# Nine rooms for the raw weight pieces of a gated linear attention and SwiGLU kernel, four of them fetched at once

## The chip, the cores and the metric

The kernel runs on one core of a Trainium2 chip. A time is the device time of one execution in microseconds (us); several executions of the same kernel are run and the median is told. Beside them stands one execution that was profiled: it has a time of its own, and a span, from the first to the last instruction, that is a little shorter. Everything read from a profile belongs to that one execution.

## The reference, cut to what matters

```python
# q, k, v, a_re, a_im: (4, 8, 768, 48) f32; weights arrive as float64
mag = sqrt(a_re**2 + a_im**2); scale = min(mag, 0.999) / (mag + 1e-6)
a = (a_re + 1j * a_im) * scale
for t in range(768):                       # per batch and head
    S = a[t][:, None] * S + outer(k[t], v[t])
    y[t] = q[t] @ real(S)
x = y as (3072, 384)                       # tokens x (heads * 48)
xn = x / sqrt(mean(x*x) + 1e-6) * rms_g
out = (silu(xn @ w_gate) * (xn @ w_val)) @ w_out   # 384 -> 1536 -> 384
```

## The kernel before

The 3072 tokens are 24 chunks of 128. The recurrence is computed by chunk: the running products of the gates are turned into a magnitude (products, square roots) and a phase (arctan, running sum, sine and cosine), keys and queries are scaled and rotated by them ("rot0" to "rot3": four multiplications), and then each chunk is a small attention: scores (`s_ps`, L1064), transposed keys (`kt_ps`, L1085), the carried state (`state_ps`, L1107) and outputs (`y_ps`, L1136). The output is normalised (`ss_ps` twice, a root on GpSimd, called POOL, at L1171) and written as `xT`.

Gates are computed for *units*: units 0 and 1 are one chunk each, every later unit is two chunks. After its four rotations a unit's rows are moved from one layout in SBUF to another by DMAs (L876, `kr` and `qr`; the four moves are `moved0` to `moved3`), and its first scores wait for all four. Units 0 and 1 issue their `qr` moves on the POOL queue, all else goes on SP's queue.

The feed-forward works on *groups* of two chunks. A gate tile ("tile" in the text: `gv_ps`, L1212) is six matmuls with a gate weight and six by a value weight as the profile counts them; ACT applies silu to the one half (L1216) and VectorE, called DVE, multiplies (`hT<-gv_ps`, L610). There are twelve tiles in a group, 144 in all, and three PSUM buffers for them. Groups 0 and 1 are projected by `wo` directly (L1239), later ones with seven products instead of eight (L1290), whose weight sums `combine` computes.

The weights arrive in 64-bit form and are narrowed in the kernel. They come in 18 *pieces* of 768 KB: pieces 0 to 11 are, in turn, gate and value weights of six column blocks (two tiles need the two pieces of a block), pieces 12 to 17 are `wo`. `fetch` (L944) issues a DMA for each on the POOL queue into a *room*; `narrow` (L976) turns it into f32 with one ACT instruction ("share", L991) and three on VectorE ("shifted" L996, "signed" L613, "total" L610). A room is free again when its piece is narrowed. Rooms are slices of buffers that are not in use yet: before, 0 and 1 in the first `hT` buffer, 2 and 3 in the second, 4 and 5 in a tensor `rooms`. Between fetches POOL copies one element of an earlier piece (L971) or of a moved row (L968), so that the queue waits until that has landed: pieces 0 to 2 go at once, piece 3 waits for unit 0's last move, piece 4 for unit 1's, and each later one for the piece two before it.

The order of everything is written out ahead of time by `Order`. Each activity (scores, gates of a unit, narrowing of even pieces, of odd pieces, and so on) is a *lane* of steps, with the engine, an assumed duration and the names that it needs. At each turn the planner takes the step that can start first by its assumed clock, plus a penalty for its lane (`late`), plus a penalty for an ACT table load if one is needed. The engines then execute their lists strictly in this order. Where the planner expects TensorE (called PE) to be idle it puts filler matmuls there (`busy`, L642), which keep the clock up and compute nothing. `BEHIND` makes the first step of a unit's gates wait for a piece:

```python
BEHIND = {3: ("piece", 7)}
yield E("ACT", ac_us(n1), [K("re"), BEHIND.get(u)] + earlier(u, "rot"), begin, K("s0"))
```

Of the kernel before, what the change touches and what calls it, by code (L numbers as in the profile page):

```python
# [45 lines left out]
class Order:  # L46
# [8 lines left out]
    HOP = 0.06  # L55
    ISSUE = 0.6
    LAND = 2.2
    RATES = {"POOL": 0.15, "SP": 0.14}
    MOVE = 2.0
    GAP = 2.5  # L60
    WARM = 3.0
    MOST = 9.0
# [24 lines left out]
    def run(self):  # L87
        while self.lanes:
            best = None
            for lane in list(self.lanes):  # L90
                if lane[2] is None:
                    lane[2] = next(lane[0], None)
                    if lane[2] is None:
                        self.lanes.remove(lane)
                        continue
                found = self.begin(lane[2], lane[1])
                if found is None:
                    continue
                table = lane[2][4].get("table")
                switch = self.TABLE if table and self.table not in table else 0.0  # L100
                if best is None or found[0] + switch < best[0]:
                    best = found[0] + switch, found[1], switch, lane
            if best is None:
                assert not self.lanes, [x[2][:3] for x in self.lanes]
                return
            _, at, switch, lane = best
            engine, us, _, emit, more = lane[2]
            lane[2] = None
            self.gap = 0.0
            if engine == "PE" and (self.fill is None or self.fill not in self.ends):  # L110
                self.gap = min(at - self.clock.get("PE", 0.0), self.MOST)
                if more.get("fills") and self.gap > 1.5:
                    self.dense = self.WARM
            emit()
            pool, n = more.get("takes", (None, 0))
            if n:
                self.free[pool] = sorted(self.free[pool])[n:]
            if switch:
                self.table = more["table"][-1 if self.table == "silu" and "sigmoid" in more["table"] else 0]
            if engine == "PE":  # L120
                if at - self.clock.get("PE", 0.0) > self.GAP and not (more.get("fills") and self.gap):
                    self.dense = 0.0
                slow = self.dense < self.WARM
                self.dense += us if more.get("dense") else 0.0
                us = us * (1.9 if slow else 1.0)
            self.clock[engine] = end = at + us + switch
            if "mb" in more:
                queue = "POOL" if engine == "POOL" else "SP"
                self.moved[queue] = max(self.moved.get(queue, 0.0), at + 0.4) + more["mb"] / self.RATES[queue]
                end = self.moved[queue] + self.LAND  # L130
            end += more.get("then", 0.0)
            for k in more.get("ends", ()):
                self.ends[k] = end
            if "gives" in more:
                self.free[more["gives"]].append(end)


def step(engine, us, needs, emit, **more):
    return engine, us, needs, emit, more
# [429 lines left out]
def fast(tc, ctx, qT, kT, v, a_re, a_im, w_gate, w_val, w_out, rms_g, out, H, bad):  # L569
# [8 lines left out]
    ND = DM // P  # L578
# [5 lines left out]
    NU = len(units)  # L584
# [18 lines left out]
    order = Order()  # L603
    tt_us = lambda n: 0.07 + n / 960
    ts_us = lambda n: 0.07 + n / 1920
    ac_us = lambda n: 0.19 + n / 1200
# [89 lines left out]
    ends = consts.tile([P, NU, ND, UC], FP32, name="ends")  # L696
# [4 lines left out]
    FW = 2 * P  # L701
    NW = DF // FW
    wg = consts.tile([P, NW, ND, FW], FP32, name="wg")
    wv = consts.tile([P, NW, ND, FW], FP32, name="wv")
    wo = consts.tile([P, NF, DM], FP32, name="wo")
    gcol = consts.tile([P, ND], FP32, name="gcol")
    hT = [consts.tile([P, NF, T], FP32, name="hT%d" % i) for i in range(2)]
# [49 lines left out]

    BEHIND = {3: ("piece", 7)}  # L760
    LATE = 0.9
    WO = 0.5

    def gates(some):
        def E(engine, us, needs, emit, *names, **more):
# [100 lines left out]
    def move_rows():  # L866
        for u, (first_, m) in enumerate(units):
            t, two = UN[u], {}

            def move(i, t=t, u=u, two=two, first_=first_, m=m):  # L870
                name, rows = ("kr", "qr")[i % 2], (1 - i // 2) * D
                queue = nc.gpsimd if u < ASIDE and i % 2 else nc.sync
                if i < 2:
                    two[name] = sized(unit, name, H, m, p=D2)
                for j in range(ND):
                    queue.dma_start(out=two[name][rows + j * L:rows + (j + 1) * L],  # L876
                                      in_=t[("ks", "qs", "k", "q")[i]][:, j])
                for n in range(m) if i == 3 else ():
                    w = slice(n * C, (n + 1) * C)
                    U[first_ + n].update(k=two["kr"][:, :, w], q=two["qr"][:, :, w])  # L880

            for i in range(4):
                aside = u < ASIDE and i % 2
                yield step("POOL" if aside else "SP", 3 * order.ISSUE,
                           [("rot%d" % i, u), ("y", units[u - 1][0] - 1) if u > 1 else None],
                           lambda i=i, move=move: move(i), mb=0.2 * m, then=order.MOVE,
                           ends=[("moved%d" % i, u)] + [("moved", u)] * (i == 3))

    def decays():
# [21 lines left out]
    parts = []  # L911
# [3 lines left out]
    raws, rooms = {}, {}  # L915
    EARLY = len(parts)

    def room(i):

        two = (0, 1) if i < 2 else (2, 3) if i < 2 * NW and i % 4 > 1 else (4, 5)  # L920
        k = two[i % 2]
        before = rooms.get(k)
        rooms[k] = i
        if k > 3:
            return raw2[k - 4], before
        return (hT[k // 2].rearrange("p f t -> p (f t)")[:, k % 2 * ND * 2 * FW:][:, 0:ND * 2 * FW]
                .rearrange("p (j f) -> p j f", j=ND).bitcast(I32)), before

    def words(raw):
# [7 lines left out]

        yield step("SP", 0.5, [("moved3", 0)], get, mb=0.01, ends=["gains"])

    FIRST, AHEAD = 2, 2  # L940
    BACK = {3: (0, "moved3"), 4: (1, "moved3")}
    landed = {}

    def fetch():  # L944
# [31 lines left out]
    def narrow(some):  # L976

        for i in some:  # L980
            to, ap, _, _ = parts[i]
            if ap.dtype == FP32:
                yield step("NONE", 0.0, [("raw", i)], lambda: None, ends=[("piece", i)])
                continue
            n = to.shape[1] * to.shape[2]
            to = to.rearrange("p c f -> p (c f)")
            part = {}

            def share(i=i, to=to, part=part, n=n):
                part["lo"], part["hi"] = words(raws.pop(i))  # L990
                nc.scalar.activation(out=to, in_=part["lo"].bitcast(U32), func=AF.Copy, bias=2.0,  # L991
                                     scale=2.0 ** -51)
                part["t"] = stage.tile([P, n], I32, tag="t", name="t")

            def shifted(part=part):
                nc.vector.tensor_scalar(out=part["t"], in0=part["hi"], scalar1=3, scalar2=None,  # L996
                                        op0=ALU.logical_shift_left)

            def signed(to=to.bitcast(I32), part=part):
                stt(to, part["hi"], -2 ** 31, to, ALU.bitwise_and, ALU.bitwise_or)  # L1000

            def total(to=to.bitcast(I32), part=part):
                tt(to, part["t"], to, ALU.add)

            more = dict(late=lambda i=i: (0.2 if i < 2 * NW else 0.3 if ("xT", 3) in order.ends else WO)
                        if ("rot", 1) in order.ends else LATE)
            yield step("ACT", 0.05 + ac_us(n), [("raw", i)], share, ends=[("share", i)], **more)
            yield step("DVE", tt_us(n), [("raw", i), ("piece", i - 2) if i > 1 else None], shifted, **more)
            yield step("DVE", tt_us(n), [("share", i)], signed, ends=[("both", i)], **more)
            yield step("DVE", tt_us(n), [], total, ends=[("piece", i)], **more)  # L1010
# [189 lines left out]
    def feed_forward(groups):  # L1200
        for g in groups:
            t = G[g]
            for f in range(NF):
# [15 lines left out]
                    tt(t["hT"][:, f], t["gv", f][:, 1], t["hT"][:, f])  # L1219

                w_ = [("piece", 2 * (f * P // FW) + i) for i in range(2)]
                free = [("piece", 2 * NW - 1) if g == 1 else None, ("out", g - 2) if g > 1 else None] if f == 0 else []
                yield step("PE", 12 * pe_us(T), w_ + free + [("xT", g * UC + UC - 1)], tile_, then=0.2, dense=True, fills=True,
                           ends=[("gv", g, f)] + [("up", g)] * (f == NF - 1), takes=("g", 1))
                yield step("ACT", ac_us(T), [("gv", g, f)], silu, table=["silu"], ends=[("silu", g, f)])
# [4 lines left out]
            for i in range(UC):  # L1230
                n = g * UC + i
# [120 lines left out]
    order.lane(feed_forward(range(0, NG, 2)), 0.02)  # L1352
    order.lane(feed_forward(range(1, NG, 2)), 0.03)
    order.lane(gates([0]), 0.05)
    order.lane(gates(range(1, NU)), 0.2)
    order.lane(gains(), 0.1)
    order.lane(fetch(), 0.2)
    order.lane(narrow(range(0, len(parts), 2)), 0.1)
    order.lane(narrow(range(1, len(parts), 2)), 0.3)
    order.lane(combine(), 0.15)  # L1360
    order.lane(small(), 0.5)
    order.fill = ("up", 1)
    with tc.manual_schedule():
# [66 lines left out]
```

## Time and profile before

| | |
|---|---|
| median of 10 runs | 771.56 us (768.85 to 777.26) |
| the profiled execution | 770.83 us, span 769.1 us, mean granted clock 0.984 |
| PE busy | 714.4 us (93%) |
| VectorE busy | 474.0 us (62%) |
| ACT busy | 342.5 us (45%) |
| POOL busy | 49.2 us (6%) |
| chain that ended last | PE 82%, DMA 6%, DVE 5% |
| largest groups of matmuls | `gv_ps` 211.6 + 214.3 us, `out_ps` L1290 85.9 + 42.8 us |
| weight pieces | 768 KB each, 7.6 to 9.2 us from issue to landing (medians) |

Busy time of PE includes the filler matmuls. PE, VectorE and ACT each execute their list in order, so an instruction that waits holds up all that stand behind it on its engine. A time in brackets behind a row of the timeline is the idle time before it and what ended it. Numbers with "x" count instructions of the profile; it shows a float32 matmul as two.

### The profile page before, as it was taken

How to read it: one execution, taken by the hardware profiler on the slowest of the kernel's cores; microseconds unless marked ns; L12 is line 12 of the kernel's file. 1: busy time of each engine (PE TensorE's matmuls, PEld its weight loads, DVE VectorE, ACT ScalarE, POOL GpSimd, SP SyncE). 2: the span in 40 equal slices, each digit the busy share in tenths (PEclk: the TensorE clock that was granted, in tenths of full speed). 3: DMA queues.
4: the chain of work that ended last, by engine and by line, in shares of the span. 5: the costliest groups of instructions: out<-in, count | busy, mean ns of one | idle time of the engine just before them, and what ended most of it. 6: DMA issues, size and time to landing. Idle time of an engine off the chain costs nothing.

```text
span 769.1 us, 12742 instructions
## 1 busy us (share of the span) xinstructions
PE 714.4 (93%) x5082; PEld 631.9 (82%) x5082; DVE 474.0 (62%) x887; ACT 342.5 (45%) x570; POOL 49.2 (6%) x94
## 2 busy tenths in 40 slices
PE   0479899799999999999999999999999999999995
PEld 0265788696788999999999989999889999899985
DVE  4888599668575975877486677768427442522121
ACT  6655385735646555475645656555211111111110
POOL 3430230100000000000000000000000000000000
PEclk9989999989999999999999999999999999999998
DMA  7791980941909247091905629072654344300000
GB/s 233 99 269 28 215 246 15 206 129 36 180 14 125 62 53 154 16 153 53 151 23 80 127 38 149 22 101 66 79 146 143 98 153 146 100 1 21 11 10 26
DMA packets 103331, 76.53 MB, mean 100 GB/s; under 512 B 39328, under 2 KB 98464, under 8 KB 103264
## 3 DMA queue, kind: packets, MB, share of 16 engines
q1 hardware_dynamic: 98656, 60.30, 40.5%
q0 software_dynamic: 3744, 14.94, 6.9%
q8 instruction: 42, 0.69, 0.4%
q10 hardware_dynamic: 864, 0.39, 0.2%
q14 instruction: 25, 0.20, 0.1%
HBM read 51.98 MB, written 4.76 MB: 74 GB/s over the span
## 4 chain that ended last, share of the span: by engine, by line
PE 82%; DMA 6%; DVE 5%; issue 1%; ACT 1%; SPq 1%; POOL 0%; DVEq 0%; ACTq 0%
PE gv_ps L1212 44%; PE out_ps L1290 18%; PE s_ps L1064 6%; PE y_ps L1136 5%; PE out_ps L1239 4%; PE state_ps L1107 3%; DMA qr<-q 3%; DMA kr<-k 2%; PE kt_ps L1085 2%; DMA qr<-qs 1%; PE ss_ps L1174 1%; SPq L876 1%; DVE re L840 1%; PE gv_ps L642 0%; PE ss_ps L1162 0%
## 5 line engine op out<-in xcount | busy, mean ns | idle before, releaser
L1212 PE MATMUL gv_ps<-xT,wv 128*128 128x256 f32 x864 | 211.6, 381 | 2.9 <-DVE wv L610 2.9
L1212 PE MATMUL gv_ps<-xT,wg 128*128 128x256 f32 x864 | 214.3, 384 | 0.0
L1212 PEld LDWEIGHTS gv_ps<-xT,wv 128*128 128x128 f32 x864 | 165.2, 191 | 25.9 <-DVE wv L610 3.3
L1212 PEld LDWEIGHTS gv_ps<-xT,wg 128*128 128x128 f32 x864 | 161.7, 192 | 23.8 <-issue 4.3
L610 DVE TENSOR_TENSOR hT<-gv_ps,hT 128x256 f32<-128x256 f32 x144 | 60.3, 421 | 181.3 <-ACT hT L1216 180.8
L1216 ACT ACTIVATE hT<-gv_ps 128x256 f32<-128x256 f32 x144 | 54.9, 383 | 252.7 <-PE gv_ps L1212 252.5
L1290 PE MATMUL out_ps<-wo,hT 128*128 128x192 f32 x480 | 85.9, 329 | 1.2 <-ACT ot L1312 1.2
L1290 PEld LDWEIGHTS out_ps<-wo,hT 128*128 128x128 f32 x480 | 78.3, 190 | 3.1 <-ACT ot L1312 1.9
L1064 PE MATMUL s_ps<-qr,kr 96*128 96x128 f32 x384 | 50.7, 288 | 9.6 <-DMA qr<-q 5.7
L1064 PEld LDWEIGHTS s_ps<-qr,kr 96*128 96x128 f32 x384 | 48.0, 201 | 11.3 <-issue 6.1
L1171 POOL TENSOR_TENSOR rs<-ssq,mhalf 128x1 f32<-128x1 f32 x24 | 16.7, 694 | 518.4 <-DVE ssq L1166 518.4
L1290 PE MATMUL out_ps<-rooms,S 128*128 128x192 f32 x240 | 42.8, 328 | 0.7 <-DVE ot L610 0.7
L1312 ACT COPY ot<-out_ps 128x192 f32<-128x192 f32 x40 | 12.7, 318 | 65.7 <-PE out_ps L1290 65.7
L1290 PEld LDWEIGHTS out_ps<-rooms,S 128*128 128x128 f32 x240 | 39.5, 190 | 2.0 <-DVE ot L610 1.2
L1069 DVE TENSOR_TENSOR am<-s_ps,causal 128x512 f32<-128x512 f32 x48 | 31.8, 685 | 9.1 <-PE s_ps L1064 8.6
L610 DVE TENSOR_TENSOR ot<-out_ps,ot 128x192 f32<-128x192 f32 x30 | 10.7, 356 | 34.7 <-PE out_ps L1290 22.3
L1239 PE MATMUL out_ps<-wo,hT 128*128 128x384 f32 x96 | 31.8, 486 | 0.0
L1061 PE MATMUL s_ps<-ks,ident 128*128 128x384 f32 x14 | 6.9, 666 | 26.3 <-DVE ks L610 26.3
L1216 ACT ACT_TABLE_LOAD x24 | 30.8, 1283 | 0.4
L1107 PEld LDWEIGHTS state_ps<-vz,kt 128*96 128x96 f32 x320 | 29.8, 165 | 1.0 <-issue 0.5
L1107 PE MATMUL state_ps<-vz,kt 128*96 128x48 f32 x320 | 29.9, 246 | 0.0
L613 DVE SCALAR_TENSOR_TENSOR xT<-y_ps,gcol,rb 128x128 f32<-128x128 f32 x72 | 20.7, 343 | 13.8 <-PE gv_ps L1212 9.7
(132 smaller groups left out, 917.7 us busy)
## 6 DMA issues: line engine op xcount, KB each, us to landing
k<-in_k_dram SPq DMA_DIRECT2D x24, 192.0 KB, 3.6
q<-in_q_dram SPq DMA_DIRECT2D x24, 192.0 KB, 3.3
vz<-in_v_dram SPq DMA_DIRECT2D x24, 192.0 KB, 3.6
rooms<-in_w_out_dram POOLq DMA_DIRECT2D x6, 768.0 KB, 7.6
out_dram<-ot SPq DMA_DIRECT2D x24, 192.0 KB, 2.2
again<-in_w_gate_dram SPq DMA_DIRECT2D x12, 384.0 KB, 3.4
again<-in_w_val_dram SPq DMA_DIRECT2D x12, 384.0 KB, 4.3
again<-in_w_out_dram SPq DMA_DIRECT2D x12, 384.0 KB, 3.1
```

The source lines that it names most:

```text
L610: nc.vector.tensor_tensor(out=o, in0=x, in1=y, op=op)
L613: nc.vector.scalar_tensor_tensor(out=o, in0=x, scalar=c, in1=y, op0=op0, op1=op1, **kw)
L1064: nc.tensor.matmul(u["s_ps"][a][:, h], lhsT=u["k"][:, a * HH + h], rhs=u["q"][:, a * HH + h], start=True, stop=True)
L1069: nc.vector.tensor_tensor(out=u["am"][a], in0=u["s_ps"][a], op=ALU.mult, in1=causal.unsqueeze(1).to_broadcast([C, HH, C]))
L1085: nc.tensor.transpose(u["kt_ps"][a][:, h], u["k"][:, a * HH + h], ident[0:D2, 0:D2])
L1107: nc.tensor.matmul(u["st_ps"][:, h], lhsT=u["kt"][h // HH][:, h % HH], rhs=u["v"][:, h, 0:D], start=True, stop=True)
L1136: nc.tensor.matmul(u["y_ps"][32 * p:32 * (p + 1), i // 4], lhsT=columns(left, i, odd), rhs=right(2 * (i // 3) + odd), start=side == 0 and ...
L1171: nc.gpsimd.tensor_tensor(out=u["rs"], in0=u["ssq"], in1=mhalf, op=ALU.pow)
L1212: nc.tensor.matmul(ps[:, i], lhsT=w_[:, f * P // FW, d, cols], rhs=t["xT"][:, d], start=d == 0, stop=d == ND - 1)
L1216: nc.scalar.activation(out=t["hT"][:, f], in_=t["gv", f][:, 0], func=AF.Silu)
L1239: nc.tensor.matmul(t["o_ps", i], lhsT=t["hT"][:, f, i * C:(i + 1) * C], rhs=wo[:, f], start=f == 0, stop=f == NF - 1)
L1290: nc.tensor.matmul(at["ps"][to] if name in ("P7", "P5", "P3", "P4") else at["ps"][:, to], lhsT=left[:, f], rhs=b[:, f], start=start and f ...
```

## The change

- Nine rooms instead of six: two in the first `hT` buffer (6 and 7 now), two in the second (0 and 1), two in `rooms` (2 and 3), and three in `wo` (4, 5 and 8), which is not written until the `wo` pieces are narrowed. Pieces 0 to 11 take rooms 6, 7, 0, 1, 2, 3, 4, 5, 8, 0, 1, 2; later ones alternate between 3 and 2. A `wo` piece is narrowed only after the pieces in the `wo` rooms are.
- Pieces 0 to 3 are fetched at once (`FIRST`); piece 4 waits only for piece 2 to land; piece 5 waits for unit 1's last move.
- Unit 2's gates begin behind piece 3, unit 3's behind piece 9 (7 before).
- Pieces 0 to 3 are narrowed with a penalty of 0.02, the later gate and value pieces with 0.1 (0.2 before).
- The first group waits for the pieces of its own two rooms, the second likewise.
- The planner assumes a faster POOL queue, longer moves, and counts a table load at half its time when it chooses; `combine` has a smaller penalty.

```diff
-    RATES = {"POOL": 0.15, "SP": 0.14}
-    MOVE = 2.0
+    RATES = {"POOL": 0.19, "SP": 0.14}
+    MOVE = 3.0
...
-                if best is None or found[0] + switch < best[0]:
-                    best = found[0] + switch, found[1], switch, lane
+                if best is None or found[0] + 0.5 * switch < best[0]:
+                    best = found[0] + 0.5 * switch, found[1], switch, lane
...
-    BEHIND = {3: ("piece", 7)}
-    LATE = 0.9
+    BEHIND = {2: ("piece", 3), 3: ("piece", 9)}
+    LATE = 0.6
     WO = 0.5
+    EAGER = 4
...
-                           lambda i=i, move=move: move(i), mb=0.2 * m, then=order.MOVE,
+                           lambda i=i, move=move: move(i), mb=0.2 * m, then=order.MOVE * m,
...
+    ROOM = dict(enumerate((6, 7, 0, 1, 2, 3, 4, 5, 8, 0, 1, 2)))
+
     def room(i):
-        two = (0, 1) if i < 2 else (2, 3) if i < 2 * NW and i % 4 > 1 else (4, 5)
-        k = two[i % 2]
+        k = ROOM.get(i, 2 + (i + 1) % 2)
         before = rooms.get(k)
         rooms[k] = i
-        if k > 3:
-            return raw2[k - 4], before
-        return (hT[k // 2].rearrange("p f t -> p (f t)")[:, k % 2 * ND * 2 * FW:][:, 0:ND * 2 * FW]
+        if k in (2, 3):
+            return raw2[k - 2], before
+        t, at = (hT[1], k) if k < 2 else (hT[0], k - 6) if k in (6, 7) else (wo, k - 4 if k < 6 else 2)
+        return (t.rearrange("p f t -> p (f t)")[:, at * ND * 2 * FW:][:, 0:ND * 2 * FW]
                 .rearrange("p (j f) -> p j f", j=ND).bitcast(I32)), before
...
-    FIRST, AHEAD = 2, 2
-    BACK = {3: (0, "moved3"), 4: (1, "moved3")}
+    FIRST, AHEAD = 3, 2
+    BACK = {5: (1, "moved3")}
...
-            more = dict(late=lambda i=i: (0.2 if i < 2 * NW else 0.3 if ("xT", 3) in order.ends else WO)
+            more = dict(late=lambda i=i: (0.02 if i < EAGER else 0.1 if i < 2 * NW else 0.3 if ("xT", 3) in order.ends else WO)
                         if ("rot", 1) in order.ends else LATE)
-            yield step("ACT", 0.05 + ac_us(n), [("raw", i)], share, ends=[("share", i)], **more)
+            there = [("piece", x) for x in range(2 * NW) if ROOM[x] in (4, 5, 8)] if i >= 2 * NW else []
+            yield step("ACT", 0.05 + ac_us(n), [("raw", i)] + there, share, ends=[("share", i)], **more)
...
-                free = [("piece", 2 * NW - 1) if g == 1 else None, ("out", g - 2) if g > 1 else None] if f == 0 else []
+                free = ([("piece", x) for x in range(2 * NW) if ROOM[x] in ((6, 7), (0, 1))[g]] if g < 2 else [("out", g - 2)]) if f == 0 else []
...
-    order.lane(gates(range(1, NU)), 0.2)
+    order.lane(gates(range(1, NU)), 0.1)
...
-    order.lane(narrow(range(0, len(parts), 2)), 0.1)
+    order.lane(narrow(range(0, len(parts), 2)), 0.3)
...
-    order.lane(combine(), 0.15)
+    order.lane(combine(), 0.05)
```

## The prediction

> **What bounds the kernel now.** I read the page first (busy time and slices), then TensorE's waits late and its timeline early, then VectorE's and the POOL queue's timelines for what released it. The slices (the last rows are the granted clock and the DMA share):
>
> ```profile
> PE   0479899799999999999999999999999999999995
> ...
> PEclk9989999989999999999999999999999999999998
> DMA  7791980941909247091905629072654344300000
> ```
>
> PE is below 9 tenths only in the first eight slices (154 us) and the last. PE's waits from 160 us to the end:
>
> ```profile
> PE out_ps L1290 <- ACT ot L1312: 1.2, 4, 0.5
> PE out_ps L1290 <- DVE ot L610: 0.7, 2, 0.5
> PE ss_ps L1174 <- POOL rs L1171: 0.6, 1, 0.6
> ```
>
> That is 2.5 us in 609. So after 160 us PE bounds, and what is won or lost before then reaches the end one for one, as long as later units' scores keep ahead. PE's timeline, 55 to 180 us (start, duration, what, idle before):
>
> ```profile
> 60.22 2.05 PE L1212 MATMUL gv_ps<-xT,wg 128*128 128x256 f32 x6
> ...
> 65.99 8.75 PE L642 MATMUL gv_ps<-causal,ident 128*128 128x512 f32 x20
> 74.57 1.46 PE L1212 MATMUL gv_ps<-xT,wg 128*128 128x256 f32 x6
> 78.89 2.93 PE L1212 MATMUL gv_ps<-xT,wv 128*128 128x256 f32 x6 [2.86 <-DVE wv L610]
> ...
> 94.34 2.02 PE L1064 MATMUL s_ps<-qr,kr 96*128 96x128 f32 x16 [1.21 <-DMA qr<-q]
> ...
> 119.49 1.46 PE L1212 MATMUL gv_ps<-xT,wg 128*128 128x256 f32 x6
> ...
> 147.96 1.46 PE L1212 MATMUL gv_ps<-xT,wv 128*128 128x256 f32 x6
> 153.91 3.78 PE L1064 MATMUL s_ps<-qr,kr 96*128 96x128 f32 x16 [4.49 <-DMA qr<-q]
> 157.48 2.77 PE L1212 MATMUL gv_ps<-xT,wg 128*128 128x256 f32 x6
> ```
>
> Two tiles (a tile is 12 matmuls, 2.59 us at full clock), 8.6 us of filler, a wait for piece 3, a wait for unit 2's rows, and the largest loss, unit 3's: 4.6 us idle, then scores in 3.57 instead of 1.8 and a tile in 4.1 instead of 2.6: 7.9 us. Why, from the VectorE, POOL and chain views:
>
> ```profile
> 77.87 0.96 DVE L610 CUSTOM_DVE_ANT_0 wv<-t,wv 128x1536 uint16<-128x1536 uint16 x1
> ...
> 132.84 0.94 DVE L610 TENSOR_TENSOR ks<-k,s 128x768 f32<-128x768 f32 x1
> ```
> ```profile
> 78.75 0.81 POOL L962 DMA_DIRECT2D hT<-in_w_val_dram  x1 [21.71 <-issue]
> ```
> ```profile
> 135.93 5.50 DMA qr<-qs
> 141.45 12.42 DMA qr<-q
> ```
>
> Piece 3 is narrowed at 78.8; piece 7's fetch, which reuses its room, stood 21.7 us for that. So pieces 7 to 9 land on unit 2's moves, VectorE has some 8 us of gaps at 81 to 92, and narrowing is pushed among unit 3's gates, whose rotations start at 132.84; its last move lands 21 us later (141.45 + 12.42).
>
> **The change, part by part.** What waits for what is from the changed program's order of instructions, durations from rows of before.
>
> *Start.* Four pieces are fetched; POOL issues one DMA more (0.77) 14 us before unit 0's moves need it. Pieces 0 and 2 are narrowed ahead of the rotations of units 0 and 1, and ACT gets two more table loads (1.28 each). Unit 0's phase sums end at 22.1 as before; shifted, signed and total (0.5, 0.9, 0.9) and two steps of unit 1 now come next: rotations at 26.4 (25.6). Unit 1's remaining eight steps then go to 31.7, piece 2's three to 34.8: rotations at 34.8 (31.86). Piece 4 is now issued on POOL between the two units' moves, at about 31.4. What it costs them no row shows: nothing if it only uses gaps, its own 768 KB at the 340 GB/s that the first fetches had, 2.3 us, if the moves stop meanwhile; I take 1, as it goes to the tail of one unit and the head of the other. First scores 38.6 (36.84), second 46.0 (43.38).
>
> A move alone took 5.50 (the chain's qr<-qs) and one beside two fetches 12.42. The Trainium skill (DMA: Bandwidth & Descriptors, Queues, rings and completion order) says that a DMA engine goes round its queues packet by packet. By it the moves would run at half pace while the fetch flows, and the 1 would be the full 2.3, the time 765.3.
>
> *First tile.* From second scores to first tile before took 16.8 us (43.38 to 60.22), 3.4 of them filler (two instructions). The same chain follows here, with the narrowing of piece 4 and unit 2's scan ahead of the second mean (ssq 58.4, rs 59.6, xT 61.5), and one filler instruction, 1.8: **62.0**, so +1.8.
>
> *Unit 2.* BEHIND puts its gates after piece 3; rotations start at 77.2 (73.38). PE no longer cares: four tiles run to 73.0 (first 3.2, then 2.59 each), the filler (same 8.6) to 81.6. Tile 5 waits for piece 5, whose signed and total stand behind the rotations and piece 10's (80.7 + 0.5 + 4 x 0.87 = 84.6). With its second half slow, tiles 5 to 8 end at 94.2, two filler instructions 1.8, scores at 96.0. Moves, issued over 8.3 us from 78.2, have landed by about 92: pieces 8 to 11 came at 57 to 77, where the DMAs idled. At 94.34 before had 7 tiles, here 8 at 96.0: 96.0 - 94.34 - 2.59 = **-0.9** so far.
>
> *Unit 3's gates ahead of the masks.* This is a new wait. ACT stands at piece 12's share until it lands (issued when piece 5 frees the room, 84.7, plus 8.3, the median of these fetches: 93). Behind it on ACT: tile 7's silu, a table load, unit 3's y, y2, r, p, two range steps and tile 8's silu (to 102.7), then the kt copies (103.5). In VectorE's order unit 3's im, w and scan (97.7, 99.1, 100.1 to 102.0) precede unit 2's masks. So PE stands inside the second chunk's scores from 100.4 to 102.7, and state follows at 103.6. From there: tile 9, y at 109.5; second state waits for ACT's kt copies, 112; second y 115.3; tile 10 118.1. Tile 11 starts at 118.4 (119.49): the stalls cost about what before spent on its 1.9 wait and 2.6 filler. Sum **-1.1**. In before a wait of 2.86 was followed by six matmuls in 2.93 instead of 1.46: I add **+1.5** for the clock (0 to 3.3, what unit 3's wait cost).
>
> On that the Trainium skill (TensorE: Matmul & The Clock Gate, Part 1) says that the clock halves after an idle window of about 3.4 us, the windows running free. By it a 2.3 us wait costs nothing, and the 1.5 would be 0, the time 762.5. The row shows that 2.86 sufficed once, so I keep it.
>
> *Unit 3's scores.* BEHIND names piece 9 and the gates start at 89.4 (90.0). More is narrowed by then and the gaps are filled, so VectorE reaches w (L610, p by r) at 109.2 (119.45), the phase sums at 118.4 (125.56), rotations at 124.9 (132.84). Fetches 15 and 16 still fall into its moves: at worst 21 us as before, 146; alone, 1536 KB at 140 GB/s is 11 us, 136. PE gets to these scores after tiles 11 to 19 and half an out-projection: 118.4 + 9 x 2.59 + 3.9 + 0.4 = 146.0, without a wait. Scores to 147.9, tiles 20 and 21 to 153.1. Before had the same work done at 161.5 (157.48 + 4.1). Sum **-8.4**, with the clock -6.9.
>
> *Later.* The rest is rearranged: out-projection halves alternate with tiles, the combine step is earlier, scores are placed 4 us later after their moves (MOVE x m is 6, was 2). There are 144 tiles and 17 filler instructions in both. Unit 4's rotations move up too (about 176 for 188). I price it at nothing: cover is VectorE at 62% and ACT at 45%, and no wait over 0.6 shows after 160; if that cover fails, each of nine units may lose a stall of its own (0 to 0.6 each, 5 at most).
>
> The profiled execution took 770.83 (span 769.1), 0.7 below the median of 771.56. 770.83 - 6.9 = **764.0**.
>
> **Rivals.** (1) *Given back.* Piece 12 takes 11.9 us as the slowest fetch here did (+3.6, all behind ACT's wait), or the filler and piece 5 keep unit 2 as it was; the gain falls to 1 to 3.3: 767.5 to 770. For: ACT is strictly in order and the fetch meets unit 2's last moves. Against: nothing else is on the queue then. That moving fetches is hidden altogether, so nothing moves, ends here too.
> (2) *Slower: the gate chain carries its delay.* Unit 2's rotations are 3.8 later; if unit 3's inherit that and its moves take 20 us again, its scores wait until 157.7 with 19 tiles done instead of 153.9 with 20: 3.8 + 2.6 = +6.4, 777. It decides once unit 3's last move lands after 151.3 + 3.9 = 155.2. For: VectorE is busy 92.1 of the 110 us from 20 to 130. Against: its 8 us of gaps at 81 to 92 are what the change fills.
>
> **How the numbers follow.** About 0.5%, 3.9 us, is what a measurement of this kernel can tell from no change. Forecast (gain over 3.9): 0.64; given back: 0.20; slower: 0.16. Low end: no clock loss (-1.5), no delay of the first moves (-1), piece 12 in 6.6 us (-1.7): 759.5. The high end goes through the given-back case and into the slower one, 773.
>
> **What would show it.** Right: no wait of scores on a move near 146 to 154; the first tile near 62; tiles 3 and 4 ahead of the filler; unit 3's rotations near 125; a wait of PE near 100 of some 3 us. Wrong: unit 3's rotations at or after 132, pieces 5 or 12 landing much later, or PE waits over 1 us after 160.

## The result, and the profile after

The changed kernel takes 767.35 us (median of 14 runs, 765.51 to 771.94), against 771.48 for the kernel before over 51 runs: a ratio of 0.9941, 95% interval 0.9919 to 0.9962. Run again beside other kernels on another occasion (e8 below) it came to 0.9932 (0.9905 to 0.9959). So it is faster by 0.4 to 0.8%, about 4.5 us; the prediction said 764.0, a gain of 6.9 on the profiled execution of before. The profiled execution of after took 765.20 us, 5.6 less than that of before, with a span of 763.4.

The slices of the page after:

```profile
PE   0388889999999999999999999999999999999995
...
PEclk9988989999999999999999999999999999999999
DMA  7798860935609209127165083172820925335300
```

PE is at 9 tenths from the seventh slice on (before from the ninth, with a 7 in the eighth, where unit 3's scores waited). The granted clock is below 9 in the third, fourth and sixth slice (the last at 95 to 115 us); before it was so in the third, in the ninth, behind that wait, and in the last. PE's waits from 160 us to the end:

```profile
PE out_ps L1296 <- ACT ot L1318: 0.7, 2, 0.5
PE out_ps L1296 <- DVE ot L610: 0.5, 1, 0.5
```

That is 1.2 us for 2.5. PE's timeline (start, duration, what, idle before):

```profile
62.84 2.41 PE L1218 MATMUL gv_ps<-xT,wg 128*128 128x256 f32 x6
...
74.14 8.75 PE L642 MATMUL gv_ps<-causal,ident 128*128 128x512 f32 x20
82.73 1.46 PE L1218 MATMUL gv_ps<-xT,wg 128*128 128x256 f32 x6
86.29 1.56 PE L1218 MATMUL gv_ps<-xT,wv 128*128 128x256 f32 x6 [2.11 <-DVE wv L610]
...
97.19 2.02 PE L1070 MATMUL s_ps<-qr,kr 96*128 96x128 f32 x16
...
104.88 1.35 PE L1070 MATMUL s_ps<-qr,kr 96*128 96x128 f32 x8 [3.22 <-DVE am L1075]
106.02 2.69 PE L1113 MATMUL state_ps<-vz,kt 128*96 128x48 f32 x16
108.51 2.89 PE L1218 MATMUL gv_ps<-xT,wg 128*128 128x256 f32 x6
111.19 2.12 PE L1218 MATMUL gv_ps<-xT,wv 128*128 128x256 f32 x6
...
150.81 1.95 PE L1070 MATMUL s_ps<-qr,kr 96*128 96x128 f32 x16
```

The steps are those that were forecast: tiles 3 and 4 stand ahead of the filler, unit 2's scores have no wait, a new wait of 3.2 us for masks comes at 101.7, and unit 3's scores at 150.8 have none (before: 4.49). The new wait, though, is followed by matmuls at a lower clock: `state_ps` in 2.69 for 1.48, and a tile in 4.7 instead of 2.6. What released it, from ACT's and VectorE's timelines:

```profile
95.31 0.91 ACT L996 ACTIVATE wo<-rooms 128x768 f32<-128x768 uint32 x1 [2.98 <-DMA rooms<-in_w_out_dram]
...
100.28 0.94 ACT L793 ACTIVATE p<-r,ones 128x768 f32<-128x768 f32 x1
```
```profile
101.25 0.96 DVE L613 SCALAR_TENSOR_TENSOR w<-s,p 128x768 f32<-128x768 f32 x1 [0.25 <-ACT p L793]
102.24 2.00 DVE L808 TENSOR_TENSOR_SCAN p<-w,zero 128x128 f32<-128x128 f32 x6
104.16 1.26 DVE L1075 TENSOR_TENSOR am<-s_ps,causal 128x512 f32<-128x512 f32 x2
```

ACT stands 2.98 us for piece 12; unit 3's p, w and scan follow; and unit 2's masks stand behind the scan on VectorE.

Unit 3's first rotation, and SP's first step behind its last move (SP stands there until that has landed), from VectorE's and SP's timelines:

```profile
129.69 0.95 DVE L610 TENSOR_TENSOR ks<-k,s 128x768 f32<-128x768 f32 x1
```
```profile
150.08 0.90 SPq L741 DMA_DIRECT2D q<-in_q_dram  x2
```

What took the wait away is the distance from the rotations to the scores. PE came 16.6 us after the first rotation before (149.4 less 132.84) and comes 21.1 after it now; the moves took 21.0 and take 20.4. The 21.1 is the same in all four executions of this list (after, e6 to e8), also in e8, where the rotations start at 133.7, later than in the kernel before.

**Where the time went.** Both programs give PE the same work in another order. To compare them at equal work I give each matmul the mean distance to its successor that its kind has in these traces without waits, give the filler nothing, and read when PE had done 30 us of that work (the first seven tiles, shortly before unit 2's scores) and 100 us (some 20 us after unit 3's). The last column is PE's last matmul less the second time.

| kernel | at 30 | at 100 | between | from 100 to the last |
|---|---|---|---|---|
| before | 92.8 | 176.1 | 83.3 | 585.5 |
| after | 92.8 | 172.6 | 79.8 | 582.8 |

So nothing came from the first 93 us, 3.5 us from the stretch with the two stalls, and 2.7 us from the 585 us after it, which the prediction had priced at nothing.

### The profile page after: what moved, and what is told of

Its sections match the earlier page's. It is cut to its first block, busy times and chain, and to the rows that moved or that the text cites. A ratio compares the mean times of both kernels' runs of the same rounds, so it can differ in the third digit from the quotient of the medians.

```text
span 763.4 us, 12722 instructions
## 1 busy us (share of the span) xinstructions
PE 711.2 (93%) x5082; PEld 631.7 (83%) x5082; DVE 473.4 (62%) x887; ACT 349.3 (46%) x573; POOL 53.3 (7%) x93
## 4 chain that ended last, share of the span: by engine, by line
PE 87%; DVE 3%; DMA 2%; ACT 1%; issue 1%; POOL 0%; ACTq 0%; POOLq 0%
PE gv_ps L1218 48%; PE out_ps L1296 18%; PE s_ps L1070 5%; PE y_ps L1142 5%; PE out_ps L1245 4%; PE state_ps L1113 3%; PE kt_ps L1091 1%; DMA rooms<-in_w_out_dram 1%; DMA qr<-q 1%; PE ss_ps L1180 1%; DVE p L808 1%; PE ss_ps L1168 0%; DVE wg L610 0%; POOL qr L877 0%; DVE am L1075 0%
## 5 line engine op out<-in xcount | busy, mean ns | idle before, releaser
L1177 POOL TENSOR_TENSOR rs<-ssq,mhalf 128x1 f32<-128x1 f32 x24 | 21.3, 886 | 522.3 <-DVE ssq L1172 522.3
L610 DVE TENSOR_TENSOR ot<-out_ps,ot 128x192 f32<-128x192 f32 x30 | 10.7, 357 | 30.2 <-PE out_ps L1296 18.2
L1067 PEld LDWEIGHTS s_ps<-ks,ident 128*128 128x128 f32 x14 | 3.3, 246 | 30.0 <-issue 28.9
## 6 DMA issues: line engine op xcount, KB each, us to landing
rooms<-in_w_out_dram POOLq DMA_DIRECT2D x6, 768.0 KB, 8.0
```

The lines of the kernel that those rows point to most:

```text
L610: nc.vector.tensor_tensor(out=o, in0=x, in1=y, op=op)
L1067: nc.tensor.matmul(flat(u["s_ps"][a])[:, 0:ND * C], lhsT=ident, rhs=rotated, start=True, stop=True)
L1177: nc.gpsimd.tensor_tensor(out=u["rs"], in0=u["ssq"], in1=mhalf, op=ALU.pow)
```

## The experiments

The theory after the comparison: the gain is unit 3's wait and the slow clock behind it, won by earlier narrowing; piece 12's share on ACT takes part of it back through the new stall. The rivals: the planner's numbers make the gain; the stall has another cause; unit 3's moves are what bounds the changed kernel.

### Dependencies added to the plan: four misses

Each of the first four kernels adds one name that a step waits for. The planner then writes all that follows anew.

```diff
# e1: the changed kernel, piece 12's share behind the transposed keys
+            there += [("kt", 2, 1)] if i == 2 * NW else []
# e2: the changed kernel, fetch 15 behind unit 3's last move (e3: both; e4: the same in the kernel before)
-    BACK = {5: (1, "moved3")}
+    BACK = {5: (1, "moved3"), 15: (4, "moved3")}
```

> The changed kernel with one name more that piece 12's ACT share waits for: the transposed keys of unit 2's first chunk. So ACT no longer stands at piece 12's fetch (2.98 us idle up to 95.31 in the changed kernel) ahead of unit 3's gate steps. Theory (that wait delays unit 3's phase scan and behind it unit 2's masks, and so makes PE's 3.2 us stall and the slow state and tile after it): the second pair of masks is done by about 101 instead of 104.2, PE's wait for them is under 1 us, state takes about 1.5 instead of 2.69 and tile 9 about 2.6 instead of 5.0; unit 3's rotations start near 127 instead of 129.7. PE then reaches unit 3's scores near 145 and may wait 1 to 4 us for their moves, so that of the 6 to 7 us only 2 to 4 stay: 763.5 to 765.5, against 767.4 for the changed kernel. Rival A (the stall has another cause, VectorE's own queue): masks stay at 103.5 or later and the time at 767 +- 1. Rival B (nothing before unit 3's scores counts, since their moves set the time): the stall goes, but the wait at the scores takes all of it back, 766.5 to 767.5.

Measured: 0.9996 (0.9971 to 1.0021), the whole gain lost. PE's timeline of e1:

```profile
105.01 1.16 PE L1071 MATMUL s_ps<-qr,kr 96*128 96x128 f32 x8 [0.18 <-DVE am L1076]
106.01 1.48 PE L1114 MATMUL state_ps<-vz,kt 128*96 128x48 f32 x16
...
156.23 2.08 PE L1071 MATMUL s_ps<-qr,kr 96*128 96x128 f32 x8 [2.99 <-DVE am L1076]
158.10 2.69 PE L1114 MATMUL state_ps<-vz,kt 128*96 128x48 f32 x16
160.59 2.64 PE L1219 MATMUL gv_ps<-xT,wg 128*128 128x256 f32 x6
```

The stall is gone where it was aimed at (0.18 for 3.22, state at 1.48) and has come back one unit later: in the new plan unit 4's scan (153.59 to 155.5 on VectorE) stands ahead of unit 3's masks, with a like wait; `state_ps` behind it takes 2.69 as there, and the tile 3.9. The theory holds for the cause and fails for the time, since the edit changed the plan behind it.

> The changed kernel, with the fetch of piece 15 (and so of 16 and 17 behind it on POOL's queue) kept until unit 3's last move has landed. Theory: unit 3's moves, alone on the DMA engines, land near 143 instead of 150.0, but PE comes to those scores at 150.8 and has no wait there, so the moves are not late in the changed kernel and nothing is won: 767 +- 1.5, at most a wait of PE for the last output weights near 165 to 175. Rival (unit 3's moves bound the changed kernel): 764 to 765. In both cases the moves should take 11 to 14 us from the first issue instead of 19; if they still take 19, fetches are not what slows them.

> The changed kernel with both: piece 12's share behind the transposed keys of unit 2's first chunk, and the fetch of piece 15 behind unit 3's last move. Theory (two limits of nearly equal size meet at unit 3's scores: the stall near 100 and the moves; only together they give their full price): no PE wait over 1 us near 100 and none at unit 3's scores, 21 tiles and the scores done near 151 to 152 instead of 157.9, time 760 to 762.5. Rival (late output weights): pieces 15 to 17 then land near 150 to 168 and PE waits for them or runs short of work near 165 to 175, which takes 3 or more back: 764 to 768.

> The kernel before (six rooms, its order, its planner numbers) with one edit: the fetch of piece 15 (16 and 17 behind it) waits for unit 3's last move. Theory (what the change won is unit 3's wait of 4.5 us and the slow clock after it, 7.9 us, by whatever means; the move's 12.4 us come from fetches 15 and 16 beside it): unit 3's moves land near 146 instead of 153.9, PE gets there at 149.4 or a little later and does not wait, 21 tiles with the scores are done near 153.6 instead of 161.5, time 763.5 to 766.5 if the later output weights cost nothing. Rival A (the earlier narrowing is what the gain comes from, by freeing VectorE): 771 +- 1.5. Rival B (the late output weights take the place of the wait): PE waits 3 us or more near 165 to 180 for pieces 15 to 17, 768 to 773.

Measured: e2 1.0105 (1.0066 to 1.0145), e3 1.0091 (1.0057 to 1.0126), e4 1.0098 (1.0063 to 1.0133); all slower, by 7 to 8 us. From PE's and POOL's timelines of e3:

```profile
191.03 2.93 PE L1246 MATMUL out_ps<-wo,hT 128*128 128x384 f32 x4 [9.38 <-DVE wo L610]
```
```profile
178.34 0.75 POOL L967 DMA_DIRECT2D rooms<-in_w_out_dram  x1 [8.54 <-DVE wo L613]
```

The late output weights decide: piece 17 is fetched at 178.3 (e2: 176.7; changed kernel: 146.8), and PE waits 9.4 us for it (e2: 5.8). In e4 PE comes to unit 3's scores at 155.95 without a wait, as the theory said, and the stretch from 30 to 100 takes 81.5 us (83.3 before); but from 100 on it takes 592.4 instead of 585.5, with waits of 2.5 us (for what ACT does late), 1.3 (for an output piece) and 3.1 (unit 4's scores, for a DMA). Rival B, the late output weights, comes nearest; its range ended at 773, and the kernel took 779.9 (772.8 for before beside it). One thing is useful here: unit 3's moves, alone, take 14.8 (e4) and 16.1 us (e2) from the first rotation until SP goes on behind them, 20.4 in the changed kernel and 21.0 before. So the fetches cost them 4 to 6 us, not the 8 I had taken.

### The same plan with smaller fetches

To take a wait away without a new plan, the next kernels keep every engine's list and shrink only a DMA; the piece's other words are what the room held before, so these kernels leave out a part of the output weights.

```diff
# SLIVER = (15, 16) in the kernel before (e5); (12,) and (12, 15, 16) in the changed kernel (e6, e7)
+                n = n // 16 if i in SLIVER else n
-                queue.dma_start(out=to, in_=...[:, c, f:f + n])
+                queue.dma_start(out=to[:, :, 0:n], in_=...[:, c, f:f + n])
```

> The kernel before, every engine's list exactly as it was; only the DMAs of pieces 15 and 16 bring a sixteenth of their columns (that part of the output weights is left out of the computation). So unit 3's moves have the DMA engines nearly to themselves, and no step is planned elsewhere. Theory (fetches 15 and 16 are what makes unit 3's moves take 21 us from the first rotation, and the wait and the slow clock that follow cost 7.9 us): the last move lands 12 to 14 us after the first rotation, about 146; PE gets to unit 3's scores at 149.4 and does not wait; scores 1.8 and the tile after them 2.6 us; ratio to before 0.988 to 0.992 (762.5 to 765.5 at 771.5 before). Rival A (the moves are slow by themselves): they still take 19 to 21 us and the ratio is 0.999 to 1.001. Rival B (what is won there is lost at the next wait): the wait goes but the ratio stays above 0.995.

> The changed kernel, every list as it was; only the DMA of piece 12 brings a sixteenth of its columns (that part of the output weights is left out of the computation). So ACT does not stand for it. Theory (piece 12's landing delays unit 3's scan and so unit 2's masks): ACT's 3 us wait goes, the second masks are done about 3 us earlier after unit 2's scores (4 us after them instead of 7), PE's stall there falls from 3.2 to under 1 us and with it the slow state and tile (5 to 6.5 us in all). PE then meets unit 3's moves, which fetches 15 and 16 still slow, and waits 1 to 3 us: of the 5 to 6.5 us 1 to 4 stay, ratio to before 0.989 to 0.993 against 0.994 for the changed kernel. Rival A (the stall has another cause): masks and stall stay, 0.993 to 0.995. Rival B (no wait at unit 3's moves): the whole 5 to 6.5 us stay, 0.986 to 0.988.

> The changed kernel, every list as it was; pieces 12, 15 and 16 are fetched to a sixteenth (that part of the output weights is left out of the computation). Theory (the stall near 100 and unit 3's moves are the two limits): no wait at either, the last move of unit 3 lands 12 to 14 us after its first rotation instead of 20, ratio to before 0.985 to 0.988, about 760 to 762.5. Rival (other work is the next limit at once, VectorE's list above all): a new wait of PE of 2 us or more between 100 and 170, ratio 0.990 or more.

> The changed kernel itself, for a second profiled execution beside the others and a ratio under the same conditions: 0.994 (0.992 to 0.996). Its first 65 us should vary by some 2 us (the runs before it show first tiles from 62.8 to 66.6 us with the same lists up to there); the stall of PE near 100 and the missing wait at unit 3's scores should be as before, each within 0.5 us. If the stall or the wait depends on the execution, the price of each step is only known as a mean.

| kernel | ratio to before, 95% | at 30 | at 100 | between | from 100 to the last |
|---|---|---|---|---|---|
| e5, before, 15 and 16 small | 0.9925 (0.9888 to 0.9963) | 97.7 | 174.9 | 77.2 | 585.5 |
| e6, after, 12 small | 0.9894 (0.9854 to 0.9934) | 94.1 | 170.5 | 76.4 | 582.8 |
| e7, after, 12, 15, 16 small | 0.9878 (0.9834 to 0.9921) | 96.6 | 172.4 | 75.8 | 582.8 |
| e8, after again | 0.9932 (0.9905 to 0.9959) | 96.8 | 176.5 | 79.7 | 582.8 |

With one plan the last columns repeat to a tenth: 79.8 and 79.7 for the two executions of the changed kernel, 582.8 for all four of its plan, 585.5 for both of the plan before. What differs from one execution to the next is the first 95 us, by up to 5 us. The seven kernels with the changed kernel's lists up to there (after, e1 to e3, e6 to e8) reach 30 us of work at 92.8 to 96.8, mean 95.2; the three with before's (before, e4, e5) at 92.8 to 97.7, mean 95.6. So what the change does up to there neither wins nor loses anything measurable by itself.

*Before, 15 and 16 small (e5).* The stretch falls from 83.3 to 77.2: unit 3's wait and its slow clock, taken away alone, are worth 6.1 us in the trace and 0.75% in the ratio, about as much as the whole change. The scores' row there:

```profile
155.83 2.05 PE L1066 MATMUL s_ps<-qr,kr 96*128 96x128 f32 x16 [1.60 <-DMA k<-in_k_dram]
```

This shows the first half of the theory: that wait was there to be won, and fetches 15 and 16 make 2.9 us of its 4.5. The moves took 18.2 us instead of 21.0, not 12 to 14 (piece 14 still lay on their first part), and a wait of 1.6 us stayed (the profile puts it down to a load on the same queue; the last move landed at 155.8), without a slow clock after it.

*After, 12 small (e6).* PE's timeline:

```profile
103.48 1.16 PE L1072 MATMUL s_ps<-qr,kr 96*128 96x128 f32 x8 [0.44 <-DVE am L1077]
104.47 1.48 PE L1115 MATMUL state_ps<-vz,kt 128*96 128x48 f32 x16
...
112.81 0.35 PE L1170 MATMUL ss_ps<-ones,sq 128*128 128x1 f32 x2 [1.50 <-ACT kt L1097]
113.02 2.02 PE L1115 MATMUL state_ps<-vz,kt 128*96 128x48 f32 x16
...
148.65 1.95 PE L1072 MATMUL s_ps<-qr,kr 96*128 96x128 f32 x16
```

The wait for masks goes from 3.2 to 0.4 and `state_ps` takes its 1.48: the stall's cause is piece 12's landing, as the theory said. Part of it comes back 8 us later, where PE waits 1.5 us, by the profile for the transposed keys that ACT copies behind unit 3's gate steps, and runs slowly after it. Net 3.3 us (79.7 to 76.4) in the trace. The times agree: 764.0 us (median of 6, 763.1 to 766.1) against 768.0 for the changed kernel run beside it (e8, 12 runs, the fastest 766.1). At unit 3's scores I had expected a wait; there is none: SP shows the moves landed at 148.1, PE comes at 148.65.

*All three small (e7).* The moves land earlier (16.9 us instead of 20.6), and nothing is won by it: 75.8 for 76.4, and the two ratios are not told apart. My "two limits of nearly equal size" falls; in the changed kernel unit 3's moves are just in time (0.7 us to spare, 0.5 in e6), and of the two only the stall near 100 was worth anything.

### Which edits carry the gain

```diff
# e9: the kernel before with the planner's numbers of the change; e10: the changed kernel with those of before
-    RATES = {"POOL": 0.15, "SP": 0.14}
-    MOVE = 2.0
+    RATES = {"POOL": 0.19, "SP": 0.14}
+    MOVE = 3.0
...
+                if best is None or found[0] + 0.5 * switch < best[0]:
...
+                           lambda i=i, move=move: move(i), mb=0.2 * m, then=order.MOVE * m,
# e11: the changed kernel with
-    LATE = 0.6
+    LATE = 0.9
```

> The kernel before with the planner's numbers of the change alone (POOL rate 0.19, MOVE 3.0 and MOVE x m, half of a table load counted); rooms, fetches, gates and penalties as before. Theory (the change's gain is in the rooms and the early fetches): no gain, ratio 1.000 or more; piece 3 is still narrowed near 79, unit 3's rotations stay at 131 or later. Since this plan puts POOL's two roots of unit 3's norms ahead of the last output piece's fetch, a wait of PE for the output weights near 180 may make it 1.005 to 1.015. Rival (the gain comes from the planner's numbers): 0.992 to 0.996. Between them: of the changed kernel's gain after 160 us, 2.7 us in the first pair of profiles, a part could come from these numbers: then PE's time from the end of unit 3's scores to its last matmul is 2 to 3 us shorter than before.

> The changed kernel with the planner's numbers of before (POOL rate 0.15, MOVE 2.0 without the factor, table loads counted whole); rooms, fetches, gates and penalties as in the change. Theory (rooms and early fetches carry the gain): ratio 0.990 to 0.996, tiles 3 and 4 ahead of the filler, unit 3's rotations at 127 to 130. Its plan has unit 2's masks ahead of unit 3's scan, so the stall near 100 should be under 1 us. Rival (the planner's numbers carry it): 0.999 to 1.003.

> The changed kernel with LATE 0.9 as before instead of 0.6, which in this plan puts piece 12's share behind unit 3's y, r and p on ACT, and the masks of units 2 and 3 ahead of the next unit's scan on VectorE; output pieces and POOL's roots keep their order. Theory (the stall near 100 costs 5 us of PE's time, of which 3.4 stayed when piece 12 was fetched to a sixteenth): no wait for unit 2's masks over 1 us, no slow state and tile after it; unit 3's rotations within 1 us of the changed kernel's, and at its scores a wait of 0 to 3 us; ratio 0.988 to 0.993 against 0.993 to 0.994 for the changed kernel. Rival (each plan has a stall of this kind somewhere, and the place only moves, as it did when piece 12's share was held): 0.994 to 1.001, with a wait of PE of 2 us or more for masks or moves between 100 and 170.

| kernel | ratio to before, 95% | at 30 | at 100 | between | from 100 to the last |
|---|---|---|---|---|---|
| e9, planner's numbers alone | 1.0064 (1.0041 to 1.0087) | 95.8 | 185.5 | 89.7 | 585.0 |
| e10, all but these | 0.9913 (0.9881 to 0.9945) | 90.5 | 169.3 | 78.8 | 585.4 |
| e11, LATE 0.9 | 1.0003 (0.9976 to 1.0030) | 99.0 | 175.8 | 76.8 | 589.0 |

The gain comes with what e10 keeps of the change: rooms, early fetches, gates behind pieces and penalties, all together. Which of these carries it was not tested one by one, and rooms and fetches do not bring it under every list: e11 has them all. The planner's numbers alone lose 5 us, though not at the place I named. From PE's timeline of e9:

```profile
118.61 11.13 PE L642 MATMUL gv_ps<-causal,ident 128*128 128x512 f32 x20
```

The planner puts 20 filler matmuls there, which run partly at half clock (11.1 us for the 8.75 of the same number elsewhere) after three waits of 1.6 to 1.9 us; the later half of the stretch has no wait at all (unit 3's scores at 153.29).

e10 is not told apart from the changed kernel: its stretch is shorter by 1 us (no stall near 100; instead a wait of 3.1 us and 2.8 us of filler at 147.65), its rest as long as before's. So of the 2.7 us after 100 the change without the planner's numbers gives none (585.4), these numbers alone 0.5, and both together 2.7; 1.3 of it are the waits shown above, the rest is spread thin and stays unexplained.

e11 does what it was made for: no wait for masks, and 76.8 between, as good as e6. It loses the gain elsewhere: its start is the slowest of all (99.0; one execution, so part of it may be chance), with a wait of 3.7 us for the squares of the second mean, and its rest takes 589.0. The rival had the number right and the mechanism wrong.

No complete version tried beats the changed kernel beyond doubt; e6, which leaves out a part of the weights, shows some 3 us to be had if piece 12 landed before ACT gets to it.

## Why the prediction was right, and where it was not

The mechanism was right: unit 3's wait of 4.49 us and the slow clock behind it are gone, for the reason given, and the price is a new wait inside unit 2's scores. All twelve gate and value pieces are narrowed by 94.1 us (119.5 before), and unit 3's rotations start 36.9 us after the seventh tile in both executions of the changed kernel (40.0 before, 39.9 in e5); the forecast had PE at the scores 21.1 us after them, which is what was measured. The total was 1.3 us too good in the pair of profiles (6.9 for 5.6), and 2.4 by the ratio of all runs (4.5). That it was no further off in the pair is luck: two misses offset each other, 3.2 us less in the first 160 us, 2.7 more after it (the 0.6 that are left lie behind the last matmul: 7.6 us to the end for 7.0).

- *Start and first tile.* Rotations at 27.0 and 35.6 (26.4, 34.8), second scores at 47.9 (46.0, a wait of 1.3 for a move), first tile 62.8 (62.0). Within what one execution differs from the next: e4 and e5, with before's lists, have their first tile 5.6 and 4.8 us later than the 60.22 that all was counted from. The 1 us for piece 4 among the first moves does not show: with this start unit 0's scores come 10.4 to 10.8 us after its first rotation (before, e4, e5: 11.3 to 11.4), unit 1's 11.8 to 12.5 (11.5 to 14.0).
- *Unit 2.* Tile 5 waits until 86.3 (84.6), scores at 97.2 (96.0) with one tile more done: +0.3 instead of -0.9. The slow second half that the sum gave tile 5 did not come (1.56 us); by before's row it would have ended tile 8 at 95.1, not at 94.2.
- *Unit 3's gates ahead of the masks.* Here the sum failed. Piece 12 landed 9.5 us after its issue, not 8.3, and was issued 1.1 later (85.8): ACT went on at 95.3 instead of 93, masks came at 104.2 instead of 102.0, and the wait was 3.2 instead of 2.3. I gave its slow clock 1.5 of a range of 0 to 3.3; it took the upper end. Tile 11 starts at 123.2, where 118.4, with the clock 119.9, was forecast: 3.3 too late.
- *Unit 3's scores.* All that is behind that stall is late with it: rotations 129.7 (124.9), scores 150.8 (146.0), the work of tiles 20 and 21 and the scores done at 157.9 (153.1, with the clock 154.6), counted as the end of tile 20 at 155.3 and a tile more, since unit 3's second scores stand between the two. That is 3.7 us ahead of before instead of the 6.9 of the sum. The moves took 20.4 us, as the worst case of 21 had it.
- *Later.* Priced at nothing, with a loss of up to 5 as the only alternative; it was a gain of 2.7. The plans tried here take 582.8 to 589.0 us for it where the output weights are not late, so this term is as large as the others, and the prediction had not worked it out. No run shows where more than the 1.3 us of waits comes from.
- *The range.* The three terms of its low end (1.5, 1 and 1.7) lead to 759.8, not 759.5.

On the clock, the page that the prediction cited (the Trainium skill, TensorE: Matmul & The Clock Gate, Part 1) would have had the wait cost nothing by its idle window of about 3.4 us. The runs speak against that: 3.22 us sufficed here (3.19 in e8), and so did 1.50 in e6, while 2.11 (tile 5) and 1.60 (e5) did not. What the page says of windows that run free fits: see the last section. From the other rule cited (DMA: Bandwidth & Descriptors, Queues, rings and completion order) the prediction took half pace for the moves and a loss of 2.3 us to piece 4; no such loss shows. The rule itself fits the DMA records, but half pace does not follow from it, since the packets differ in size: see the last section.

The given-back rival (767.5 to 770, piece 12 slower than its median) is the nearest in mechanism to what took 3 us from the forecast. The slower one needed unit 3's moves to land after 155.2; they landed at 150.1.

## What to carry to other kernels

Where a program writes the engines' lists from assumed times, every edit writes a new list, and the new list can move the time by half a per cent or more at places that the edit was not meant for (e1, e9, e11). Test a cause with the list held fixed (shrink the transfer, keep the steps): e6 priced in one run the stall that e1 and e11 took away without a gain. An instruction that waits for a transfer is priced by all that stands behind it on its engine, down to the engine that sets the time, and by the slow clock after that engine's wait; and the rest of the kernel, however well hidden, is not worth nothing when its order changes.

## What the runs showed of the hardware

The granted clock is read from the windows view (stretch, its length, busy time and instructions of PE, PEld, DVE, ACT and POOL, granted clock, DMA share, GB/s); after, e6 and e8:

```profile
104.00:111.00 7.00, 6.12 (x30) 5.68 (x31) 6.40 (x12) 6.93 (x11) 0.00 (x0) 0.62 0.55 130
```
```profile
110.00:118.00 8.00, 6.50 (x111) 5.68 (x102) 6.48 (x12) 4.40 (x8) 1.21 (x1) 0.79 0.04 2
```
```profile
111.00:118.00 7.00, 7.00 (x48) 5.60 (x51) 6.10 (x9) 5.38 (x7) 0.00 (x0) 0.57 0.05 12
```

In the records behind these means the clock is either full or half, and half, up to the last matmul, for 3.41, 6.83 or (e9, e3) 10.24 us: one, two or three steps of 3.41, which lie on a grid of that step within each execution. In the changed kernel half clock runs from 105.7 for 6.83 us, in e8 from 110.3 for 6.83, in e6 from 113.9 for 3.41; before it followed unit 3's wait for 6.83. So a wait that brings the slow clock costs PE, beside itself, about half of such a stretch, 1.7 or 3.4 us, and not a smooth amount: the 1.5 in the prediction was near one of the two values, and the wrong one. Which waits bring it is not settled by their length here (1.50 did, 2.11 did not), but mostly by how much of one step of the grid they leave idle. The 3.22 us put 2.6 us of idle PE into one step and the 1.50 fell into one, while the 2.11 were split into 1.04 and 1.07, and the 1.60 of e5 into 0.99 and 0.61. In the 13 traces, from 30 us to the last matmul, all 36 steps at full clock with more than 1.77 us of PE idle were followed by half clock, and none of the 2611 with less than 1.02; of the 52 between, 12 were.

Piece 12's 9.5 us were not a slow transfer: in the DMA records none of its bytes move before 89.3, 3.5 us after its issue (1.5 for piece 14 of the kernel before, beside which nothing ran), while unit 2's moves run at about 125 KB per us, and its 768 KB then come mostly within 4.5 us. Piece 15, issued into unit 3's moves at 135.4, waits until 139.4 likewise; then it runs alone, and no byte of the moves goes from 140 to 142.

Where both queues move bytes, they go packet by packet: from 145 to 147 there are 86 packets of the fetches and 74 of the moves, from 91 to 93 there are 76 and 78, and in the kernel before, from 149 to 151, 91 and 80. But a fetch's packet has 6144 bytes and a move's 1024, so the moves get about 40 KB per us there, not half of the 125 to 143 that they have alone but a third or less. In these two ways fetches 15 and 16 hold up unit 3's moves.
